# Block-sparse attention and a gated FFN on one core: 256-query attention units woven into the FFN one unit behind, probabilities as the stationary operand, tanh for sigmoid

## The chip, the cores and the metric

The kernel runs on one core of a Trainium2 chip. The time is device time in microseconds (us) of one launch, from the first to the last instruction and what the launch adds around it; the profiled execution is one such launch. A core has a TensorE (PE; its weight loads are listed apart as PEld), a VectorE (DVE), a ScalarE (ACT), a GpSimd (POOL, which here only issues loads) and a SyncE (SP, which issues stores). In some stretches TensorE was granted half of its clock, and this is said where it matters.

## The reference, cut to what matters

```python
B, H, S, D = 4, 8, 768, 64                        # attention
scores = q @ k.T / 8                              # per batch and head, 768 x 768
scores = where(mask, scores, -1e9)                # mask of 24 x 24 blocks of 32: band, edges, 3 random
attn   = exp(scores - max) / (sum + 1e-9)
x      = (attn @ v)  -> [3072 tokens, 512]        # heads side by side
gate   = 1 / (1 + exp(-(x @ w_gate)))             # 512 x 1536
out    = (gate * (x @ w_val)) @ w_out             # 1536 x 512, float32
```

Every token's FFN needs all 8 heads of that token, and nothing of other tokens. Neither kernel skips masked blocks: the mask is added in the score product by 24 extra contraction rows, so that a product has 64 + 24 = 88 rows.

## The kernel before

Attention runs head by head, then the FFN follows in six groups of 512 tokens. All operands on TensorE are fp16. In `matmul(out, stationary, moving)` the second operand is loaded as weights and the third streams past it.

```python
for b in range(B):
    for h in range(H):
        pt = ps.tile([128, S], f16, tag="pt", bufs=1)
        for o, src in ((0, q16[rb2]), (64, k16[rb2])):        # 12 transposes, 64 stationary columns
            for t in range(NJT):
                nc.tensor.transpose(pt[o : o + 64, t * 128 : (t + 1) * 128], src[:, h, t, :], ident)
        nc.vector.tensor_copy(qte[rq][0:64, :], pt[0:64, :])
        nc.vector.tensor_copy(kte[rq][0:64, :], pt[64:128, :])
        for t in range(NJT):                                  # 6 key tiles, 768 queries each
            st = ps.tile([128, 1024], f32, tag="st", bufs=2)
            nc.tensor.matmul(st[:, 0:512], ktile, qte[rq][0:88, 0:512], ...)
            nc.tensor.matmul(st[:, 512:768], ktile, qte[rq][0:88, 512:768], ...)
            nc.scalar.activation(ptile, st[:, 0:768], AF.Exp, bias=0.0, scale=SCALE)
        # one head later (phase B): v is stationary and carries a column of ones
        for i0, i1 in ((0, 512), (512, 768)):
            for t in range(NJT):
                nc.tensor.matmul(pv[:, 0:n], vex[rb2][:, h, t, :], pts[t][:, i0:i1], ...)
            nc.vector.tensor_copy(xT[kt][...], pv[0:64, 0:n])
            nc.scalar.activation(lnz[:, i0:i1], pv[64:65, 0:n], AF.Ln)      # the sums lie on one partition
        nc.scalar.activation(rz1, lnz, AF.Exp, bias=0.0, scale=-1.0)        # 1 / sum
        # one head later again (tail): spread 1/sum over 64 partitions, multiply
        nc.tensor.matmul(rbg[:, 0:n], ones464[0:1, :], rz1[:, i0:i1], ...)
        nc.vector.tensor_tensor(sl, sl, rbg[:, 0:n], op=ALU.mult)
# ... all attention done ...
for g in range(6):
    for f in range(12):
        # 4 matmuls into pg (x @ w_gate), 4 into pvv (x @ w_val), 512 columns each
        nc.scalar.activation(sg, pg, AF.Sigmoid)
        nc.vector.tensor_tensor(h_, sg, pvv, op=ALU.mult)
    # ... 4 x 12 matmuls with w_out, eviction, store
```

The softmax here doesn't subtract the row's maximum and nothing guards it: scores larger than these inputs give would overflow.

Of the kernel before, what the change touches and what calls it, by code (L numbers as in the profile page):

```python
# [13 lines left out]
ALU = mybir.AluOpType  # L15

B, H, S, D = 4, 8, 768, 64
BLK = 32
NB = S // BLK
NJT = S // 128  # L20
DM = H * D
DFF = 1536
NTOK = B * S
BIG = 1024.0
SCALE = 1.0 / 8.0
GT = 512
# [10 lines left out]
def kernel(  # L37
# [15 lines left out]
    _set_id = list(get_activation_tables(nc.m.arch)).index(  # L53
        "natural_log_exp_and_others"
    )
# [7 lines left out]
    e24_np = (np.arange(S)[None, :] // BLK == np.arange(NB)[:, None]).astype(np.float16)  # L63
# [7 lines left out]
    work = ctx.enter_context(tc.tile_pool(name="work", bufs=1))  # L71

    ident = sing.tile([128, 128], f16)
    nc.sync.dma_start(ident, ident_h.ap())
    e24 = sing.tile([NB, S], f16)
    nc.sync.dma_start(e24, e24_h.ap())
    ones464 = sing.tile([128, 64], f16)
    nc.vector.memset(ones464, 1.0)

    mb32 = sing.tile([NB, NB], f32)  # L80
    nc.sync.dma_start(mb32, mdet_h.ap())
    iota24 = sing.tile([NB, NB], f32)
    nc.sync.dma_start(iota24, iota_h.ap())
    sbi = sing.tile([NB, 3], mybir.dt.int64)
    nc.sync.dma_start(sbi, sampled_blocks)
    sbf = sing.tile([NB, 3], f32)
    nc.scalar.copy(sbf, sbi.bitcast(u16)[:, 0:12:4])
    for n in range(3):
        eqn = sing.tile([NB, NB], f32, tag=f"eq{n}", name=f"eq{n}")
        nc.vector.tensor_scalar(  # L90
            eqn, in0=iota24, scalar1=sbf[:, n : n + 1], scalar2=None, op0=ALU.is_equal
        )
        nc.vector.tensor_tensor(mb32, mb32, eqn, op=ALU.max)
    mb16 = sing.tile([NB, NB], f16)
    nc.vector.tensor_copy(mb16, mb32)  # L95

    mb24 = sing.tile([NB, S], f16)
    with tc.tile_pool(name="psmall", bufs=1, space=bass.MemoryType.PSUM) as psmall:
        p24 = psmall.tile([NB, 1024], f32)
        nc.tensor.matmul(p24[:, 0:512], mb16, e24[:, 0:512], start=True, stop=True)  # L100
        nc.tensor.matmul(p24[:, 512:768], mb16, e24[:, 512:768], start=True, stop=True)
        nc.vector.tensor_scalar(  # L102
            mb24,
            in0=p24[:, 0:768],
            scalar1=BIG,
            scalar2=BIG,
            op0=ALU.mult,
            op1=ALU.subtract,
        )

    wg = [sing.tile([128, DFF], f16, tag=f"wg{c}", name=f"wg{c}") for c in range(4)]
    wv = [sing.tile([128, DFF], f16, tag=f"wv{c}", name=f"wv{c}") for c in range(4)]
    wo = [sing.tile([128, DM], f16, tag=f"wo{f}", name=f"wo{f}") for f in range(12)]

    def _load_moe_weights():
        for c in range(4):
            nc.gpsimd.dma_start(wg[c], moe_w_gate[c * 128 : (c + 1) * 128, :])
            nc.gpsimd.dma_start(wv[c], moe_w_val[c * 128 : (c + 1) * 128, :])
        for f in range(12):
            nc.gpsimd.dma_start(wo[f], moe_w_out[f * 128 : (f + 1) * 128, :])  # L120

    xT = [sing.tile([128, NTOK], f16, tag=f"xT{c}", name=f"xT{c}") for c in range(4)]

    RQ = 4
    qte = [sing.tile([128, S], f16, tag=f"qte{r}", name=f"qte{r}") for r in range(RQ)]
    kte = [sing.tile([128, S], f16, tag=f"kte{r}", name=f"kte{r}") for r in range(RQ)]
    for r in range(RQ):
        nc.vector.tensor_copy(qte[r][64:88, :], mb24)
        nc.vector.tensor_copy(kte[r][64:88, :], e24)

    q16 = [
        sing.tile([128, H, NJT, 64], f16, tag=f"q16_{r}", name=f"q16_{r}")
        for r in range(2)
    ]
    k16 = [
        sing.tile([128, H, NJT, 64], f16, tag=f"k16_{r}", name=f"k16_{r}")
        for r in range(2)
    ]
    vex = [
        sing.tile([128, H, NJT, 65], f16, tag=f"vex{r}", name=f"vex{r}")  # L140
        for r in range(2)
    ]
    for r in range(2):
        nc.vector.memset(vex[r][:, :, :, 64:65], 1.0)

    out3 = out.rearrange("(g p) dm -> g p dm", p=128)
    CH = ((0, 512), (512, 768))

    def _moe_f(g, f, ps):
        t0 = g * GT  # L150
        pg = ps.tile([128, GT], f32, tag="pg", bufs=2)
        pvv = ps.tile([128, GT], f32, tag="pvv", bufs=2)
        for c in range(4):
            nc.tensor.matmul(  # L154
                pg,
                wg[c][:, f * 128 : (f + 1) * 128],
                xT[c][:, t0 : t0 + GT],
                start=(c == 0),
                stop=(c == 3),
            )  # L160
        for c in range(4):
            nc.tensor.matmul(  # L162
                pvv,
                wv[c][:, f * 128 : (f + 1) * 128],
                xT[c][:, t0 : t0 + GT],
                start=(c == 0),
                stop=(c == 3),
            )
        sg = work.tile([128, GT], f16, tag="sg", bufs=2)
        nc.scalar.activation(sg, pg, AF.Sigmoid)  # L170
        h_ = work.tile([128, GT], f16, tag=f"HT{f}", bufs=1, name=f"ht{f}")
        nc.vector.tensor_tensor(h_, sg, pvv, op=ALU.mult)
        return h_

    def _moe_out(g, tt, hts, ps):
        py = ps.tile([128, DM], f32, tag="py", bufs=2)
        for f in range(12):
            nc.tensor.matmul(  # L178
                py,
                hts[f][:, tt * 128 : (tt + 1) * 128],  # L180
                wo[f],
                start=(f == 0),
                stop=(f == 11),
            )
        ysb = work.tile([128, DM], f32, tag="ysb", bufs=2)
        nc.vector.tensor_copy(ysb, py)  # L186
        nc.sync.dma_start(out3[g * (GT // 128) + tt], ysb)

    pend = []
    stageB = []  # L190
    zbs = {}
    with tc.tile_pool(name="ps", bufs=1, space=bass.MemoryType.PSUM) as ps:
        for b in range(B):
            rb2 = b % 2
            for h0, h1 in (((0, 1), (1, H)) if b == 0 else ((0, H),)):
                nc.gpsimd.dma_start(
                    q16[rb2][:, h0:h1],
                    q[b, h0:h1].rearrange("h (t p) d -> p h t d", p=128),
                )
                nc.gpsimd.dma_start(  # L200
                    k16[rb2][:, h0:h1],
                    k[b, h0:h1].rearrange("h (t p) d -> p h t d", p=128),
                )
                nc.gpsimd.dma_start(
                    vex[rb2][:, h0:h1, :, 0:64],
                    v[b, h0:h1].rearrange("h (t p) d -> p h t d", p=128),
                )
            if b == 1:
                _load_moe_weights()
            for h in range(H):  # L210
                gh = b * H + h
                rq = gh % RQ
                pt = ps.tile([128, S], f16, tag="pt", bufs=1)
                for o, src in ((0, q16[rb2]), (64, k16[rb2])):
                    for t in range(NJT):
                        nc.tensor.transpose(  # L216
                            pt[o : o + 64, t * 128 : (t + 1) * 128],
                            src[:, h, t, :],
                            ident,
                        )  # L220
                nc.vector.tensor_copy(qte[rq][0:64, :], pt[0:64, :])
                nc.vector.tensor_copy(kte[rq][0:64, :], pt[64:128, :])  # L222
                pts = []
                for t in range(NJT):
                    st = ps.tile([128, 1024], f32, tag="st", bufs=2)
                    ktile = kte[rq][0:88, t * 128 : (t + 1) * 128]
                    nc.tensor.matmul(  # L227
                        st[:, 0:512], ktile, qte[rq][0:88, 0:512], start=True, stop=True
                    )
                    nc.tensor.matmul(  # L230
                        st[:, 512:768],
                        ktile,
                        qte[rq][0:88, 512:768],
                        start=True,
                        stop=True,
                    )
                    ptile = work.tile([128, S], f16, tag=f"PT{t}", bufs=3, name=f"pt{t}")
                    nc.scalar.activation(  # L238
                        ptile, st[:, 0:768], AF.Exp, bias=0.0, scale=SCALE
                    )  # L240
                    pts.append(ptile)
                def _phaseB(b=b, h=h, rb2=rb2, pts=pts, gh=gh):
                    kt, hh = h // 2, h % 2
                    lnz = work.tile([1, S], f32, tag="lnz", bufs=3)
                    for i0, i1 in CH:
# [82 lines left out]
```

## Time and profile before

| | before |
|---|---|
| time, median (lowest to highest) | 416.27 us (416.21 to 417.53, 4 runs) |
| first exponential | 15.1 us |
| one head of attention, steady | 6.27 us |
| one matmul of 512 columns in the FFN | 215 ns from start to start |

The head's 6.27 us is the distance between the first exponentials of neighbouring heads in the trace. First, the head of the profile page and its chain of waits: the work that ended last, followed back from the last instruction, as shares of the span.

```profile
span 417.8 us, 5146 instructions
PE 391.4 (94%) x2082; PEld 184.9 (44%) x2082; DVE 178.9 (43%) x307; ACT 239.7 (57%) x363; POOL 39.5 (9%) x39
PE 61%; ACT 33%; DVE 3%; issue 1%; DMA 0%; SPq 0%
```

Then the busy-time table: one stretch of attention, two between the stages and one of the FFN. The columns are the stretch, its length, and busy us (number of instructions) by engine, then TensorE's granted clock (PEclk, 1.00 is full), and what the DMAs did.

```profile
core 0: us, PE busy (x) PEld busy (x) DVE busy (x) ACT busy (x) POOL busy (x), PEclk, DMA share, GB/s
80.00:100.00 20.00, 19.40 (x123) 9.62 (x120) 10.67 (x20) 19.32 (x30) 0.00 (x0) 1.00 0.00 1
210.00:220.00 10.00, 8.49 (x31) 4.08 (x30) 2.54 (x5) 6.73 (x10) 0.00 (x0) 0.68 0.00 0
220.00:230.00 10.00, 7.32 (x23) 2.42 (x21) 3.64 (x7) 3.86 (x6) 0.00 (x0) 0.66 0.00 0
300.00:350.00 50.00, 50.00 (x233) 22.69 (x232) 17.89 (x26) 10.75 (x18) 0.00 (x0) 1.00 0.08 32
```

The two middle rows are the seam between the stages: the last exponential ends at 216.2 us, the first FFN product starts at 224.5, and the clock was half for 13.7 us between 209.6 and 230.1.

### The profile page before, as it was taken

How to read it: one execution, taken by the hardware profiler on the slowest of the kernel's cores; microseconds unless marked ns; L12 is line 12 of the kernel's file. 1: busy time of each engine (PE TensorE's matmuls, PEld its weight loads, DVE VectorE, ACT ScalarE, POOL GpSimd, SP SyncE). 2: the span in 40 equal slices, each digit the busy share in tenths (PEclk: the TensorE clock that was granted, in tenths of full speed). 3: DMA queues.
4: the chain of work that ended last, by engine and by line, in shares of the span. 5: the costliest groups of instructions: out<-in, count | busy, mean ns of one | idle time of the engine just before them, and what ended most of it. 6: DMA issues, size and time to landing. Idle time of an engine off the chain costs nothing.

```text
span 417.8 us, 5146 instructions
## 1 busy us (share of the span) xinstructions
PE 391.4 (94%) x2082; PEld 184.9 (44%) x2082; DVE 178.9 (43%) x307; ACT 239.7 (57%) x363; POOL 39.5 (9%) x39
## 2 busy tenths in 40 slices
PE   0799999999999999999987999999999999999996
PEld 0454444444444444444432444444444444444442
DVE  6445555555555555555523333333332332332431
ACT  1399999999999999999973320320321321321320
POOL 8253362002120000000000000000000000000000
PEclk9999999999999999999966999999999999999999
DMA  9999999900997000000000002002002002002002
GB/s 86 145 147 160 213 169 154 69 2 0 147 55 26 1 2 0 2 0 2 0 0 0 2 1 102 0 0 102 0 2 100 1 2 100 0 2 100 0 2 100
DMA packets 80614, 20.84 MB, mean 50 GB/s; under 512 B 74936, under 2 KB 76496, under 8 KB 80592
## 3 DMA queue, kind: packets, MB, share of 16 engines
q0 software_dynamic: 76848, 14.16, 58.9%
q1 hardware_dynamic: 3744, 6.37, 4.0%
q8 instruction: 16, 0.26, 0.3%
q14 instruction: 6, 0.05, 0.0%
HBM read 28.39 MB, written 6.29 MB: 83 GB/s over the span
## 4 chain that ended last, share of the span: by engine, by line
PE 61%; ACT 33%; DVE 3%; issue 1%; DMA 0%; SPq 0%
PE pg L154 15%; PE pvv L162 15%; PE py L178 15%; ACT lnz L260 6%; PE st L227 6%; PE pv L249 3%; PE rbg L268 2%; PE pt L216 2%; PE st L230 2%; DVE xT_119 L278 1%; DMA e_64<-bb_e 0%; DVE eq_76 L90 0%; DVE mb_85 L95 0%; DVE mb_87 L102 0%; ACT pt_2203 L238 0%
## 5 line engine op out<-in xcount | busy, mean ns | idle before, releaser
L170 ACT ACTIVATE sg<-pg 128x512 f16<-128x512 f32 x72 | 43.0, 597 | 134.5 <-PE pg L154 134.5
L186 DVE COPY ysb<-py 128x512 f32<-128x512 f32 x24 | 16.6, 691 | 45.2 <-PE py L178 45.2
L249 PEld LDWEIGHTS <-vex_141 128*65 128x65 f16 x192 | 22.0, 115 | 18.1 <-issue 8.4
L260 ACT ACTIVATE lnz<-pv 1x512 f32<-1x512 f32 x64 | 27.5, 474 | 3.1 <-DVE xT_119 L256 2.4
L154 PE MATMUL pg<-xT_116,wg_96 128*128 128x512 f16 x72 | 27.8, 385 | 0.5 <-DVE xT_119 L278 0.5
L249 PEld LDWEIGHTS <-vex_140 128*65 128x65 f16 x192 | 21.4, 113 | 15.3 <-issue 5.0
L162 PE MATMUL pvv<-xT_116,wv_100 128*128 128x512 f16 x72 | 27.8, 386 | 0.0
L154 PE MATMUL pg<-xT_117,wg_97 128*128 128x512 f16 x72 | 27.8, 386 | 0.0
L154 PE MATMUL pg<-xT_118,wg_98 128*128 128x512 f16 x72 | 27.8, 386 | 0.0
L154 PE MATMUL pg<-xT_119,wg_99 128*128 128x512 f16 x72 | 27.8, 386 | 0.0
L162 PE MATMUL pvv<-xT_117,wv_101 128*128 128x512 f16 x72 | 27.6, 383 | 0.0
L162 PE MATMUL pvv<-xT_118,wv_102 128*128 128x512 f16 x72 | 27.5, 383 | 0.0
L162 PE MATMUL pvv<-xT_119,wv_103 128*128 128x512 f16 x72 | 27.5, 382 | 0.0
L227 PE MATMUL st<-qte_120,kte_124 88*128 88x512 f16 x48 | 19.8, 413 | 1.7 <-DVE kte_124 L222 1.3
L227 PE MATMUL st<-qte_123,kte_127 88*128 88x512 f16 x48 | 18.6, 388 | 0.8 <-ACT pt_2352 L238 0.2
L227 PE MATMUL st<-qte_122,kte_126 88*128 88x512 f16 x48 | 18.4, 383 | 0.5
L227 PE MATMUL st<-qte_121,kte_125 88*128 88x512 f16 x48 | 18.4, 383 | 0.4
L256 DVE CAST xT_119<-pv 64x512 f16<-64x512 f32 (+1 forms) x16 | 8.6, 550 | 17.7 <-PE pv L249 17.6
L268 PEld LDWEIGHTS <-ones_66 1*64 1x64 f16 x64 | 6.3, 101 | 21.1 <-issue 19.0
L256 DVE CAST xT_116<-pv 64x512 f16<-64x512 f32 (+1 forms) x16 | 8.5, 549 | 13.6 <-PE pv L249 13.6
L256 DVE CAST xT_117<-pv 64x512 f16<-64x512 f32 (+1 forms) x16 | 8.6, 550 | 12.7 <-PE pv L249 12.7
L256 DVE CAST xT_118<-pv 64x512 f16<-64x512 f32 (+1 forms) x16 | 8.6, 550 | 12.7 <-PE pv L249 12.7
(760 smaller groups left out, 861.8 us busy)
## 6 DMA issues: line engine op xcount, KB each, us to landing
out_dram<-ysb SPq DMA_DIRECT2D x24, 256.0 KB, 2.0
q_1_137<-in_q_dram POOLq DMA_DIRECT2D x2, 768.0 KB, 10.0
k_1_139<-in_k_dram POOLq DMA_DIRECT2D x2, 768.0 KB, 12.0
vex_141<-in_v_dram POOLq DMA_DIRECT2D x2, 768.0 KB, 11.3
q_0_136<-in_q_dram POOLq DMA_DIRECT2D x1, 768.0 KB, 9.5
k_0_138<-in_k_dram POOLq DMA_DIRECT2D x1, 768.0 KB, 12.7
vex_140<-in_v_dram POOLq DMA_DIRECT2D x1, 768.0 KB, 12.2
q_0_136<-in_q_dram POOLq DMA_DIRECT2D x1, 672.0 KB, 8.7
```

The source lines that it names most:

```text
L154: nc.tensor.matmul(pg, wg[c][:, f * 128 : (f + 1) * 128], xT[c][:, t0 : t0 + GT], start=(c == 0), stop=(c == 3),)
L162: nc.tensor.matmul(pvv, wv[c][:, f * 128 : (f + 1) * 128], xT[c][:, t0 : t0 + GT], start=(c == 0), stop=(c == 3),)
L170: nc.scalar.activation(sg, pg, AF.Sigmoid)
L178: nc.tensor.matmul(py, hts[f][:, tt * 128 : (tt + 1) * 128], wo[f], start=(f == 0), stop=(f == 11),)
L186: nc.vector.tensor_copy(ysb, py)
L216: nc.tensor.transpose(pt[o : o + 64, t * 128 : (t + 1) * 128], src[:, h, t, :], ident,)
L227: nc.tensor.matmul(st[:, 0:512], ktile, qte[rq][0:88, 0:512], start=True, stop=True)
L230: nc.tensor.matmul(st[:, 512:768], ktile, qte[rq][0:88, 512:768], start=True, stop=True,)
L249: nc.tensor.matmul(pv[:, 0:n], vex[rb2][:, h, t, :], pts[t][:, i0:i1], start=(t == 0), stop=(t == NJT - 1),)
L256: nc.vector.tensor_copy(xT[kt][hh * 64 : hh * 64 + 64, b * S + i0 : b * S + i1], pv[0:64, 0:n],)
L260: nc.scalar.activation(lnz[:, i0:i1], pv[64:65, 0:n], AF.Ln)
L268: nc.tensor.matmul(rbg[:, 0:n], ones464[0:1, :], rz1[:, i0:i1], start=True, stop=True,)
```

## The change

Four things at once, by its intent:

1. Attention works in units of 256 queries of one batch (12 units), four head pairs each, six key tiles (slots) per pair. The FFN of a unit becomes possible when its four pairs are done; its matmuls are dealt out between the slots of the units that follow, by a running credit of 0.65 us of FFN per slot.
2. In the value product the probabilities are stationary (128 keys by 128 queries) and v streams past (65 columns). The sums then lie one to a query partition, so that a reciprocal and a multiplication on VectorE normalise. The logarithms, the one-partition exponential and the broadcast product fall away; x has to be transposed instead.
3. sigmoid(z) = 0.5 (1 + tanh(z/2)), so that one activation table serves for all.
4. Token p·6+t stands in partition p, tile t, so that loads read 1536 contiguous bytes in place of 256.

The order of instructions is fixed by hand. Core of the diff (declarations, loads and mask cut):

```diff
-    _set_id = list(get_activation_tables(nc.m.arch)).index("natural_log_exp_and_others")
+    _set_id = list(get_activation_tables(nc.m.arch)).index("exp_and_others")
...
+    def prep(src, dst, b, p, t0=0, t1=NT, evac=None):
+        pr = work.tile([128, NT, 2, D], f16, tag="pr", bufs=3, name="pr")
+        nc.vector.tensor_copy(pr[:, t0:t1, :, :], src[...].rearrange("a h t d -> a t h d"))
+        tp = ps.tile([128, 1024], f16, tag="m", bufs=2, name="tpq")
+        for t in range(t0, t1):
+            nc.tensor.transpose(tp[...], pr[:, t, :, :], ident)          # both heads of the pair at once
+        for a in range(2):
+            nc.vector.tensor_copy(dst[b % 2][0:D, 2 * p + a, ...], tp[a * D : (a + 1) * D, 0:n])
...
+    def qk(b, u, p, t):
+        st = ps.tile([128, 2, UQ], f32, tag="s", bufs=3, name="st")
+        # 2 matmuls of 256 columns, then exp of 128 x 512
+        nc.scalar.activation(pt, st, AF.Exp, bias=0.0, scale=SCALE)
...
+        def pv(self, i):                                                  # i = 0..3: query half, head
+            for t in range(NT):
+                nc.tensor.matmul(
+                    self.acc[:, s, a, :],
+                    self.pts[t][:, a, s * 128 : (s + 1) * 128],
+                    vex[self.b % 2][:, 2 * self.p + a, t, :], ...)
+        def norm(self):
+            nc.vector.reciprocal(rz, self.acc[:, :, :, D : D + 1])
+            nc.vector.tensor_tensor(self.x16, self.acc[:, :, :, 0:D], rz.broadcast_to(...), op=ALU.mult)
...
+        # FFN: th = tanh(pg[:, 0] / 2);  ht = (th + 1) * pg[:, 1];  y * 0.5 at the eviction
+                self.py = ps.tile([128, DM], f32, tag="y", bufs=1, name="py")
...
+    for p in range(NP):                                                   # all four pairs before the first score
+        mask_rows(0, 2 * p, 2 * p + 2)
+        prep(k16, kT, 0, p)
+        prep(q16, qT, 0, p, 0, 2)
+        vcopy(0, 2 * p, 2 * p + 2)
...
+            for t in range(NT):
+                pts.append(qk(b, u, p, t))
+                # t = 1..4: value product of the pair before;  t = 0: transpose of the pair before that
+                if t in (2, 5) and todo:
+                    todo.popleft()()                                      # prepare the next batch
+                give(0.65)                                                # FFN of the unit behind
```

## The prediction

> **What bounds the kernel now.** Two stages in series. In the busy-time table, every 20 us from 40 to 200 us has ScalarE busy 19.1 to 19.3 us: attention is ScalarE-bound. There the chain of waits alternates exponentials (0.81 us, 128x768), two logarithms (0.59, 0.36 us) and a one-partition exponential (0.82 us); the last three cost 57 us for 32 heads. From 230 to 415 us TensorE never idles: 300 to 350 us holds 233 matmuls, 215 ns per 512 columns, so 864 FFN matmuls need 186 us, while ScalarE is idle 134 us (sigmoid waiting for the gate product).
>
> **What the change does.** It fills TensorE's slack in attention with the FFN; TensorE becomes the one limit.
>
> - ScalarE, per unit of 256 queries: 24 exponentials of 128x512 (0.60 us by the sigmoid of that size) and 12 tanh of 128x256 (about 0.38 us): 19 us; 227 us in all.
> - TensorE: scores keep their 147,456 columns, 576x109 ns = 63 us. FFN 1152x109 ns + 288x216 ns = 188 us. Transposes 288x56 ns = 16 us. The broadcast product (10 us) goes. The value product becomes 1152 matmuls of 65 columns, each with its own 128-column weight load. The Trainium skill, "TensorE: Matmul & The Clock Gate", section on weight-path perf modes, says 128 columns of a non-FP32 type load fast; the trace agrees so far that 128-column loads take 99 ns and 65-column ones 115 ns. The pair's spacing isn't in the trace; I estimate 45 ns (35 to 65): 52 us against 62 before. Sum about 319 us.
> - VectorE: normalisation and two copies move here. About 0.42 us per slot (one key tile of one head pair), 0.9 where the next batch is prepared, against a slot of 1.07 us: not the limit, but TensorE waits for it.
>
> **The sum.**
> - Start: all four pairs' copies, transposes, evictions (0.55 us per 64x768) and mask rows precede the first score. About 4 us of VectorE per pair from about 10 us on: first exponential near 26 us (15 us before).
> - 30 slots without FFN (unit 0 and a quarter of unit 1), ScalarE/VectorE-bound: 22 us.
> - 258 slots of 0.22 scores + 0.18 value product + 0.02 + 0.65 FFN = 1.07 us: 276 us.
> - Preparing batches 1 to 3: 8 us of transposes and about 0.5 us of waiting for VectorE in each of 24: 20 us.
> - One y buffer: 12 waits of 0.5 us: 6 us.
> - Tail: the last value product, 21 us of FFN, last store: 25 us.
>
> Total about 372 us, 11% less.
>
> **What will show it.** ScalarE about 60% busy throughout; the chain of waits almost all TensorE; the last FFN unit alone at the end. Value-product spacing near 45 ns decides the largest term: 10 ns is 11 us. First exponential near 26 us. In each batch's middle unit TensorE waits for the pair copy.
>
> **What would make it wrong.** Weight loads that don't hide behind 65-column matmuls (80 ns or more: plus 40 us, still faster). A start slowed by VectorE operations stretched while the DMA descriptors are written (before, 24x24 operations took 1.8 us at 6 us). FFN weights arriving late for the first unit (14 MB by 55 us; before never exceeds 213 GB/s): plus 5 to 10 us. Weight loads wholly hidden (30 ns), few waits: 345 us.
>
> Range 348 to 396 us. Faster by over 2%: 0.96; within 2%: 0.03; slower: 0.01.

## More of the kernel before

The piece of the chain that covers one head shows that neither engine was alone on the path (columns: start, us, what):

```profile
59.53 0.81 ACT pt_642 L238
60.34 0.72 ACT rz_616 L262
61.06 0.70 ACT pt_647 L238
61.80 0.38 PE st L227
62.28 0.33 PE rbg L268
62.61 0.23 PE pt L216 x2
62.84 0.32 PE st L227
63.16 0.12 PE st L230
63.31 0.81 ACT pt_662 L238
64.12 0.77 ACT pt_667 L238
64.92 0.85 ACT lnz L260 x2
65.80 0.81 ACT pt_737 L238
```

From 61.8 to 63.3 us the path runs through TensorE: a score product, the broadcast product, transposes, scores again.

## The result

| | before | changed |
|---|---|---|
| median | 416.27 us | 371.18 us (369.34 to 371.94, 4 runs) |
| ratio | | 0.8891, 95% interval 0.8854 to 0.8928 |

Ratios here are the mean time of one kernel's fast runs over that of the other's fast runs of the same rounds, so they are not quite the ratio of the medians quoted. The changed kernel is 11% faster, at 371.18 us against 372 predicted.

The same lines of the page after the change:

```profile
span 370.2 us, 8135 instructions
PE 322.2 (87%) x3458; PEld 254.4 (69%) x3458; DVE 178.7 (48%) x458; ACT 214.6 (58%) x433; POOL 26.9 (7%) x37
PE 76%; DMA 11%; DVE 7%; POOL 2%; ACT 2%; issue 1%; ACTq 0%; POOLq 0%
```

The busy-time table, one stretch in which nothing is prepared and one in which batch 3 is:

```profile
180.00:200.00 20.00, 19.64 (x214) 15.41 (x213) 6.99 (x19) 13.75 (x28) 0.00 (x0) 1.00 0.08 28
220.00:240.00 20.00, 17.69 (x214) 15.44 (x213) 12.55 (x32) 12.78 (x28) 0.00 (x0) 1.00 0.04 15
```

ScalarE is no longer near its limit, and nothing of the two-stage picture is left. The timeline of TensorE within two slots shows the terms of the steady part (start, us, then the instructions, merged):

```profile
200.45 0.38 PE L202 MATMUL st<-qT,kT 88*128 88x256 f16 x2
200.67 0.36 PE L224 MATMUL pv<-vex,pt 128*128 128x65 f16 x6
200.87 0.60 PE L262 MATMUL pg<-xT,wv 128*128 128x256 f16 x4
201.30 0.38 PE L202 MATMUL st<-qT,kT 88*128 88x256 f16 x2
```

Two score products take 0.22 us, six pairs of weight load and value product 0.20 us (33 ns each), four FFN products 0.43 us. What interrupts this is in the table of waits for TensorE (engine, tile, line, who it waited for: us in total, times, longest):

```profile
PE tpq L184 <- DVE pr L178: 29.7, 22, 3.2
PE p L154 <- DVE mb L151: 6.5, 1, 6.5
PE py L285 <- DVE ysb L294: 6.0, 12, 0.9
```

The first line is the pair copy: 20.9 us of it fall before 51 us (start, unit 0 and the first pair of unit 1), 8.8 us in the merged part. And the start, on the timeline: the first score product waits in TensorE's queue behind the transposes of all four pairs, which wait for VectorE.

```profile
9.39 0.36 DVE L178 COPY pr<-k 128x768 f16<-128x768 f16 x1
...
14.94 0.53 DVE L178 COPY pr<-k 128x768 f16<-128x768 f16 x1
...
20.18 0.36 DVE L178 COPY pr<-k 128x768 f16<-128x768 f16 x1
...
25.12 0.43 DVE L178 COPY pr<-k 128x768 f16<-128x768 f16 x1
...
28.64 3.04 ACT L210 ACTIVATE pt<-st 128x512 f16<-128x512 f32 x6 [26.62 <-PE st L202]
```

The four pairs begin about 5.2 us apart. In this first part TensorE was slow: until 42.4 us its matmuls start 0.83 to 0.84 ns a column apart, later 0.43 to 0.49, and 0.83 again from 52.7 to 56.1 us, where half the clock is on record. The clock records begin only at 42.4 us (21.9 us in the kernel before, with the same spacing until then), so the 1.00 that the clock column prints for this part is no reading. The predicted sum against the trace, by the stretches of the prediction:

| term | predicted, us | in the trace, us | how read |
|---|---|---|---|
| start, to the first exponential | 26 | 28.6 | timeline |
| 30 slots without FFN | 22 | 22.5 | to the first score of unit 1's second pair, 51.1 us |
| 258 slots with FFN (276), preparation (20), waits for y (6) | 302 | 289.8 | to the end of the last slot's FFN, 340.9 us |
| tail | 25 | 29.3 | to the end, 370.2 us |
| sum | 375 | 370.2 | |

The terms of the prediction in fact add up to 375; its text says "about 372".

### The profile page after: what moved, and what is told of

Its sections match the earlier page's. It is cut to its first block, busy times and chain, and to the rows that moved or that the text cites. A ratio compares the mean times of both kernels' runs of the same rounds, so it can differ in the third digit from the quotient of the medians.

```text
span 370.2 us, 8135 instructions
## 1 busy us (share of the span) xinstructions
PE 322.2 (87%) x3458; PEld 254.4 (69%) x3458; DVE 178.7 (48%) x458; ACT 214.6 (58%) x433; POOL 26.9 (7%) x37
## 4 chain that ended last, share of the span: by engine, by line
PE 76%; DMA 11%; DVE 7%; POOL 2%; ACT 2%; issue 1%; ACTq 0%; POOLq 0%
PE pg L262 33%; PE py L285 17%; PE st L202 14%; PE pv L224 9%; DMA q<-in_q_dram 6%; DMA wg<-in_moe_w_gate_dram 4%; PE tpq L184 3%; DVE ysb L294 3%; DVE ht L272 2%; DMA k<-in_k_dram 2%; ACT th L271 2%; PE tpx L246 1%; DVE pr L178 1%; POOL q L101 0%; POOL wg L111 0%
## 5 line engine op out<-in xcount | busy, mean ns | idle before, releaser
L210 ACT ACTIVATE pt<-st 128x512 f16<-128x512 f32 x288 | 169.4, 598 | 103.4 <-PE st L202 102.5
L202 PE MATMUL st<-qT,kT 88*128 88x256 f16 x576 | 113.5, 281 | 0.1
L272 DVE SCALAR_TENSOR_TENSOR ht<-th,pg 128x256 f16<-128x256 f32 x144 | 60.6, 421 | 91.3 <-ACT th L271 91.1
L262 PE MATMUL pg<-xT,wg 128*128 128x256 f16 x576 | 86.9, 273 | 1.1 <-DVE xT L249 0.9
L262 PE MATMUL pg<-xT,wv 128*128 128x256 f16 x576 | 86.8, 273 | 0.0
L285 PE MATMUL py<-wo,ht 128*128 128x512 f16 x288 | 75.7, 378 | 6.0 <-DVE ysb L294 6.0
L271 ACT ACTIVATE th<-pg 128x256 f32<-128x256 f32 x144 | 55.2, 383 | 41.9 <-PE pg L262 40.0
L202 PEld LDWEIGHTS <-kT 88*128 88x128 f16 x576 | 56.9, 101 | 24.8 <-issue 1.7
L224 PE MATMUL pv<-vex,pt 128*128 128x65 f16 x1152 | 69.4, 196 | 0.0
L224 PEld LDWEIGHTS <-pt 128*128 128x128 f16 x1152 | 63.1, 99 | 6.2 <-DVE qT L188 0.4
L285 PEld LDWEIGHTS <-ht 128*128 128x128 f16 x288 | 24.3, 97 | 22.1 <-issue 7.5
L188 DVE COPY kT<-tpq 64x768 f16<-64x768 f16 x32 | 17.7, 554 | 13.4 <-PE tpq L184 13.2
```

The lines of the kernel that those rows point to most:

```text
L188: nc.vector.tensor_copy(dst[b % 2][0:D, 2 * p + a, t0 * 128 : t1 * 128], tp[a * D : (a + 1) * D, 0:n],)
L202: nc.tensor.matmul(st[:, a, :], kT[b % 2][0:KR, h, t * 128 : (t + 1) * 128], qT[b % 2][0:KR, h, u * UQ : (u + 1) * UQ], start=True, stop=True,
L210: nc.scalar.activation(pt, st, AF.Exp, bias=0.0, scale=SCALE)
L224: nc.tensor.matmul(self.acc[:, s, a, :], self.pts[t][:, a, s * 128 : (s + 1) * 128], vex[self.b % 2][:, 2 * self.p + a, t, :], start=(t == 0),
L262: nc.tensor.matmul(self.pg[:, i, :], w[:, c, f * 128 : (f + 1) * 128], self.xT[:, c, :], start=(c == 0), stop=(c == 3),)
L271: nc.scalar.activation(th, self.pg[:, 0, :], AF.Tanh, bias=0.0, scale=0.5)
```

## The experiments

Twelve kernels ran, in three sets. The changed kernel (371.18 us) is the base of most; each set ran the kernel before beside it, whose medians were 416.85, 416.83 and 416.62 us. The changed kernel was not run again, so differences to it compare with its first four runs.

### Does TensorE set the pace? Two doublings

`pv_twice` computes each value product twice:

```diff
-            for t in range(NT):
+            for t in 2 * list(range(NT)):
                 nc.tensor.matmul(self.acc[:, s, a, :], self.pts[t][...], vex[...], start=(t == 0), stop=(t == NT - 1))
```

> The changed kernel with every value product computed twice (1152 more weight loads and 65-column matmuls; the result is the same, no other engine gets work). Theory, TensorE sets the pace and a pair of weight load and matmul costs 33 ns (what the trace of the changed kernel suggests): 1152 x 33 = +38 us, 409 us. If the predicted 45 ns were right: +52 us, 423 us. Rival, ScalarE or the latency between engines sets the pace: well under 20 us more.

Measured: 403.19 us (402.14 to 403.62), ratio to before 0.9663 (0.9611 to 0.9715): 32.0 us more than the changed kernel. Divided by 1152, a pair costs 28 ns in time, a little under the 33 ns between its starts, as a part of it fills waits. A unit without preparation went from 25.0 to 27.9 us (distance of first exponentials), which is 2.9 us / 96 = 30 ns. The predicted 45 ns is refuted, and TensorE's work shows nearly whole in the time.

`tanh_twice` gives ScalarE 55 us more and TensorE nothing:

```diff
-                nc.scalar.activation(th, self.pg[:, 0, :], AF.Tanh, bias=0.0, scale=0.5)
+                for _ in range(2):
+                    nc.scalar.activation(th, self.pg[:, 0, :], AF.Tanh, bias=0.0, scale=0.5)
```

> The changed kernel with every tanh computed twice: 144 x 0.38 = 55 us more of ScalarE, no work for other engines. Theory, TensorE sets the pace in the 258 slots with FFN (ScalarE 0.79 us of a 1.12 us slot before, 0.98 with the second tanh): under 12 us more, most of it in the last unit, where the tanh lies on the path. Rival, ScalarE sets the pace of the merged part: +40 to +55 us.

Measured: 380.49 us (379.37 to 382.06), 9.3 us more for 55 us of work. In the profiled executions (7.4 us apart) the last exponential starts 5.0 us later and the stretch after it is 2.4 us longer. ScalarE doesn't set the pace; the longer path from gate product to `ht` costs a little. The two runs together decide for TensorE.

### What is the merging worth?

`serial` keeps every new piece but lets the FFN units run after all attention:

```diff
-                        f_ = Ffn(done.b, done.u, done.xT)
-                        ffn_parts.extend(f_.parts())
+                        later.append((done.b, done.u, done.xT))
...
+    for args in later:
+        ffn_parts.extend(Ffn(*args).parts())
+        give(1e6)
```

> The changed kernel with its merging undone: the FFN units run after all attention (12 buffers for x transposed in place of 3), everything else as it is. Theory, the merging is what makes the new pieces pay: 28 us start, 288 slots at about 0.62 us of ScalarE = 179, then 12 FFN units at 17.5 us (as the last unit of the changed kernel took alone) = 210: 415 to 425 us, no faster than the kernel before. Rival, the gain comes from the lighter ScalarE and TensorE work and not from the merging: 380 us or less.

Measured: 425.29 us (421.93 to 428.41; the longest run is of the slow state, the three fast ones have a median of 422.93), ratio to before 1.0169 (1.0079 to 1.026, fast runs alone): slightly slower than before, whether by 2% is unclear, and 52 us slower than the changed kernel by the fast runs. Attention lasts from 29 to 207 us, and the twelve FFN units then take 17.7 us each, with one accumulator for y (9.4 us of waits in all) and two for the gate waiting for evictions that merging hides. In the profiled run the clock was half in five stretches between 53 and 152 us, some 31 us in all; what that adds is not separated. So the new attention and the new FFN, in series, gain nothing; they gain when each fills the waits of the other. A clean attention unit in this run takes 11.6 us, 0.48 us a slot, although one exponential lasts 0.60 us: back to back they overlap. The Trainium skill, "ScalarE: Activation LUTs", section "What ACT_TABLE_LOAD costs", says that back-to-back activations overlap by about 93 ns; here it is 0.12 us (0.478 from start to start, 0.597 long). The theory counted 0.62 us a slot, and was right on the total because the units that prepare a batch took up to 19.0 us.

### Was ScalarE the limit of attention before?

`before_nolog` takes the logarithms and the one-partition exponential from the kernel before (wrong result):

```diff
-                        nc.scalar.activation(lnz[:, i0:i1], pv[64:65, 0:n], AF.Ln)
...
-                    nc.scalar.activation(rz1, lnz, AF.Exp, bias=0.0, scale=-1.0)
+                    rz1 = rconst          # memset once to 1/256
```

> The kernel before with only its two logarithms and the one-partition exponential per head taken away (wrong result on purpose: every head is scaled by a constant; the broadcast product and its multiplication stay). Theory, ScalarE bounds attention alone: a head falls from 6.27 us to about 5.0 us (6 exponentials of 0.81 = 4.9; TensorE needs about 4.8): 32 x 1.27 = 40 us less, 376 us, as much as the whole change gives. Rival, TensorE's order and waits bind as soon as ScalarE gets lighter: under 25 us less.

Measured: 404.54 us (404.38 to 404.68), ratio 0.9699 (0.9649 to 0.9749): 12 us less, not 40. The rival holds. A head falls only from 6.27 to 6.02 us (mean of two: they alternate 5.6 and 6.4), which is 8 us for 32 heads; the rest of the gain lies outside the steady heads, in the profiled executions (15.6 us apart) 2.0 us before the first exponential and 6.6 us after the last head began. The busy-time table of the same stretch:

```profile
80.00:100.00 20.00, 20.00 (x128) 10.47 (x126) 11.02 (x20) 15.12 (x21) 0.00 (x0) 1.00 0.01 1
```

And the chain of waits of the whole run:

```profile
PE 94%; DMA 3%; POOL 1%; DVE 1%; issue 0%; ACT 0%; ACTq 0%; POOLq 0%
```

ScalarE is at 15.1 of 20 and off the chain, and TensorE has taken over. But its columns explain only part of 6.02 us: scores 4608, value product 4608, transposes 1536, broadcast 768 columns are 11,520, or 4.8 us at the FFN's 215 ns for 512. Where is the rest? The timeline of TensorE in the kernel before shows it:

```profile
200.96 0.27 PE L230 MATMUL st<-qte_121,kte_125 88*128 88x256 f16 x1
201.16 0.24 PE L216 MATMUL pt<-ident,q_1_137 128*64 128x128 f16 x1
...
201.35 0.22 PE L216 MATMUL pt<-ident,q_1_137 128*64 128x128 f16 x1
201.50 0.39 PE L227 MATMUL st<-qte_121,kte_125 88*128 88x512 f16 x1
```

The score product of 256 columns is followed after 0.20 us, not 0.11, where the next matmul has 64 stationary columns, and a transpose by a score product after 0.15, not 0.06. Over 40 to 160 us of `before_nolog` the start times of consecutive matmuls give medians of 202 ns for 256-column score to transpose, against 108 to a value product, and of 152 ns for transpose to score. All changes of shape together (64-column transposes; broadcast product with one contraction row and 64 columns) are about nine a head, 93 to 116 ns each. The Trainium skill, "TensorEngine Tiling (Array Packing)", section "Tiling Modes", key properties, says that changing the tiling mode drains the TensorE; it gives no time for it. `wide_nolog` tests this: q and k side by side, one 128-column transpose for both, 128 columns of ones.

```diff
-        for o, src in ((0, q16[rb2]), (64, k16[rb2])):
-            for t in range(NJT):
-                nc.tensor.transpose(pt[o : o + 64, t * 128 : (t + 1) * 128], src[:, h, t, :], ident)
+        for t in range(NJT):
+            nc.tensor.transpose(pt[:, t * 128 : (t + 1) * 128], qk16[rb2][:, h, t, :, :], ident)
...
-    ones464 = sing.tile([128, 64], f16)
+    ones464 = sing.tile([128, 128], f16)
...
```

> The run before_nolog (kernel before without its logarithms, wrong result on purpose) with q and k side by side in one tile, so that one 128-column transpose serves both (6 a head in place of 12 of 64 columns), and the ones of the broadcast product widened from 64 to 128 columns. Theory: what kept TensorE at 6.02 us a head there is the change between matmuls with 64 and with 128 stationary columns: score to transpose starts 202 ns apart in place of 108, transpose to score 152 in place of 56, about nine such changes of 95 ns a head. Without them TensorE needs about 4.7 us and the exponentials 4.9: 5.0 us a head, 404.5 - 32 x 1.0 = 372 us. Rival, the 6.02 us come from waits between the engines (score buffers, evictions): 395 us or more.

Measured: 383.62 us (382.95 to 385.03): 20.9 us less than `before_nolog`, 5.29 us a head (mean of two: they alternate 4.6 and 6.0). TensorE now starts a transpose 0.11 us after the score product, where there were 0.20:

```profile
86.27 0.27 PE L225 MATMUL st<-qte,kte 88*128 88x256 f16 x1
86.38 0.33 PE L213 MATMUL pt<-ident,qk 128*128 128x128 f16 x3
...
87.02 0.33 PE L213 MATMUL pt<-ident,qk 128*128 128x128 f16 x3
87.28 0.28 PE L260 MATMUL rbg<-rconst,ones 1*128 1x256 f16 x1
87.49 0.41 PE L243 MATMUL pv<-pt,vex 128*65 128x512 f16 x1
```

The rival is refuted, and the theory's 372 us was too low by 12. The broadcast product still has one contraction row: the last transpose to it takes 149 ns from start to start, not 56, and it takes 208 ns to the next value product, not 109. Four such changes a head, by these figures, are about 0.4 us, which would cover the missing 0.3; that part was not tested. Part of the 0.72 us gained is the shorter row of transposes (6 in place of 12, in two column halves that partly overlap), so the run shows both together. An estimate from the traces parts them: 768 columns less are 0.32 us at the FFN's rate, and what the start-to-start times hold beyond their columns fell from 1.17 to 0.77 us a head, which is the other 0.40.

`before_wide` is the same edit with the logarithms kept and the result right.

> The kernel before, logarithms kept, with the same wide transposes and wide ones (right result). Theory: ScalarE still needs 6.2 us a head, so the lighter TensorE gains next to nothing alone: 411 to 417 us. Rival: TensorE was the tighter limit of the two, 395 us or less.

Measured: 418.22 us (416.46 to 419.84), ratio 1.0025 (0.9969 to 1.008): nothing gained, and 1 us above the expected range. Each limit hides the other: ScalarE's part alone gives 12 us, TensorE's part alone nothing, both 33 us.

### Is tanh needed, and what does the token order give?

`sigmoid` puts the sigmoid back into the changed kernel (and takes the 0.5 and the added 1 out).

> The changed kernel with the sigmoid in place of tanh (0.5 and the added 1 taken out too; right result). Theory: sigmoid and exponential don't share a table, so each change reloads one at 1.28 us, about 2 x 144 reloads when they alternate: ScalarE 215 + 370 = 585 us, and the time follows: 580 to 640 us. Rival: the reloads overlap or are grouped, under 450 us.

Measured: 668.73 us (2 runs, 667.57 and 669.90), above the expected range; the groups of instructions name the cost:

```profile
L271 ACT ACT_TABLE_LOAD x131 | 168.1, 1283 | 2.3
L210 ACT ACT_TABLE_LOAD x130 | 166.8, 1283 | 2.4
```

These are 261 reloads, 335 us of ScalarE. TensorE's granted clock averaged 0.746 over the span, which the expectation had not counted; that its waits for ScalarE brought the clock down is not shown. The Trainium skill, "ScalarE: Activation LUTs", puts a load at about 1283 ns (section "What ACT_TABLE_LOAD costs") and lists exp and tanh in one set (section "Table sets: the hidden batching unit"); the trace agrees to the nanosecond, and the changed kernel has one load in all. This merging without tanh would have lost.

`tok_natural` undoes the token order alone.

```diff
-TOK = (np.arange(S) % 128) * NT + np.arange(S) // 128
+TOK = np.arange(S)
...
-            src[b, h0:h1].rearrange("h (p t) d -> p h t d", t=NT)[:, :, t0:t1, :],
+            src[b, h0:h1].rearrange("h (t p) d -> p h t d", t=NT)...   # partial loads split by tile
...                                                                     # the store likewise
```

> The changed kernel with the token order put back: q, k and v are read in pieces of 256 bytes, not 1536 (partial q loads are split by key tile, because a load has at most three dimensions: 7 more issues). Theory: [...] batch 1, which lands at 50 us and holds TensorE there, lands 8 to 12 us later: 376 to 384 us. Rival, the loads are hidden and the start is VectorE's: under 3 us.

Measured: 378.72 us (378.03 to 379.61), 7.5 us more. In the profiled executions, which differ by 5.8 us, unit 0 begins 1.6 us later and takes 1.0 us longer, and unit 1 takes 32.2 us in place of 29.1; the rest is as long. In unit 1 the pair copy waits 1.10 us for the load of k of batch 1 and 2.21 us for that of q, where the changed kernel waits 0.20 us for q, and TensorE idles 3.41 us behind the second. The seven additional issues are part of the run, so a share of the later start may be theirs. The Trainium skill, "DMA: Bandwidth & Descriptors", specifications, names 512 bytes as the least transfer for line rate; here loads moved 203 to 206 GB/s from 20 to 60 us with 1536-byte pieces, and with 256-byte ones fell to about 155 GB/s from 47 us on, while batch 1 came in.

### Taking away the waits that are left

Three edits aim at the pair copies, the y accumulator and the start. `pr_early` issues the pair copy two slots before its transposes:

```diff
...
+                if t in (0, 3) and todo and len(todo[0]) > 1:
+                    pair_copy(*todo[0][1:])
                 if t in (2, 5) and todo:
-                    todo.popleft()()
+                    todo.popleft()[0]()
```

> The changed kernel with the pair copy on VectorE issued two slots before the transposes that read it. Theory: TensorE no longer waits 0.5 to 1.0 us for it in most of the 24 preparations of batches 1 to 3; 10 to 15 us less, 356 to 361 us. Rival: the wait is filled by what TensorE owes anyway, or comes back as a wait for the evictions of these transposes: under 4 us.

Measured: 357.98 us (356.89 to 360.05), ratio to before 0.8576: 13.2 us less than the changed kernel, as expected. TensorE's wait for pair copies in the merged part falls from 8.8 to 2.3 us; in the profiled executions (11.9 us apart) units 1 to 8 take 9.5 us less and unit 0, where the half clock ended at 37.1 us in place of 42.4, takes 2.4 us less.

`two_y` gives y a second accumulator, taken from the scores:

```diff
-        st = ps.tile([128, 2, UQ], f32, tag="s", bufs=3, name="st")
+        st = ps.tile([128, 2, UQ], f32, tag="s", bufs=2, name="st")
...
-                self.py = ps.tile([128, DM], f32, tag="y", bufs=1, name="py")
+                self.py = ps.tile([128, DM], f32, tag="y", bufs=2, name="py")
```

> The changed kernel with two output accumulators in PSUM in place of one, and two score buffers in place of three. Theory: the 12 waits for the eviction of y (0.37 to 0.78 us) go, 4 to 6 us less, 366 us, and two score buffers are enough because the exponential has a 1.1 us slot to free one. Rival: the third score buffer is needed, slower by 5 us or more.

Measured: 364.77 us (362.72 to 365.53), 6.4 us less. The wait for y is gone, and the two score buffers cost 0.5 us of waits in the whole run.

`start_order` prepares only pair 0 before the first score:

```diff
-    for p in range(NP):
-        mask_rows(0, 2 * p, 2 * p + 2)
-        prep(k16, kT, 0, p); prep(q16, qT, 0, p, 0, 2); vcopy(0, 2 * p, 2 * p + 2)
+    first_k(0); first_q(0)                  # the same for pair 0 alone
...
+            for p in range(1, NP):
+                todo.append(lambda p=p: first_k(p)); todo.append(lambda p=p: first_q(p))
...
-            todo.append(lambda: mask_rows(1, 0, H))
...  (not code: second buffer's mask rows go with batch 1, whose preparation starts in unit 1's last pair, 8 items for 12)
```

> The changed kernel with only pair 0 prepared before the first score; pairs 1 to 3 of batch 0, and the second buffer's mask rows, are prepared between the slots of units 0 to 2. Theory, the start is VectorE's queue (about 4 us for each pair): first exponential near 14 us in place of 28.6, unit 0 then bound by VectorE at about 4.2 us a pair, and FFN begins 10 to 16 us earlier; part is lost again because weights and batch 1 arrive at the same rate as before (about 204 GB/s until 63 us): 356 to 364 us. Rival, the loads set the start: under 4 us gained.

Measured: 371.79 us (369.97 to 372.37): nothing, as the rival has it, but not for its reason. The first exponential came at 13.9 us, 14.8 us sooner, and unit 2 still began 9.7 us sooner. Then it went, unit by unit (distances of first exponentials, us):

| | first exp | unit 0 | unit 1 | unit 2 | unit 3 | unit 4 | unit 5 |
|---|---|---|---|---|---|---|---|
| changed | 28.6 | 18.4 | 29.1 | 27.0 | 25.0 | 31.2 | 25.5 |
| start_order | 13.9 | 23.9 | 28.7 | 33.5 | 25.0 | 27.0 | 30.3 |
| all_three | 14.0 | 19.1 | 23.2 | 27.4 | 24.5 | 25.2 | 26.0 |

Unit 0, in which pairs 1 to 3 are now prepared, takes 5.5 us longer, and unit 2 6.6 us. From 13 to 80 us no engine that computes waited for a load, so the rival's reason is not it. In unit 2, where batch 1 is now prepared, TensorE waits 4.6 us for pair copies, in four waits; the longest, 1.94 us, stands behind mask rows in VectorE's queue:

```profile
77.75 0.55 DVE L168 COPY qT<-mb 24x1536 f16<-24x1536 f16 x1
78.23 0.54 DVE L168 COPY kT<-e 24x1536 f16<-24x1536 f16 x1
78.78 0.36 DVE L178 COPY pr<-k 128x768 f16<-128x768 f16 x1
...
79.20 0.51 PE L184 MATMUL tpq<-ident,pr 128*128 128x128 f16 x6 [1.94 <-DVE pr L178]
```

The granted clock was half from 26.1 to 39.8 us, but that does not set this run apart: by the spacing of its matmuls the changed kernel, too, ran at half rate until 42.4 us.

`all_three` puts the three edits together.

> The three edits together (start order, two y accumulators, early pair copy). Theory, they act in different stretches and add up: 371 - 11 - 5 - 10 = 345 us, 340 to 352. Rival, they overlap: 352 to 360 us.

Measured: 337.24 us (336.29 to 337.51), ratio to before 0.8072 (0.8038 to 0.8105), result right: 33.9 us less than the changed kernel, below the expected range. Alone they gave 13.2, 6.4 and -0.6, together 19.0; the remaining 14.9 is put down to the earlier start (14.7 us between the first exponentials), which is kept once the copy is early. That is by subtraction, as no run has the other two edits without it; the traces agree: unit 2 begins 16.9 us sooner than in `pr_early`, and the earlier start holds to the end. The wait of TensorE for pair copies is what fell, from 24.3 us in `start_order`:

```profile
PE tpq L191 <- DVE pr L178: 4.0, 3, 2.4
```

The clock is on record as full from 27.9 us to the end; before that the matmuls start 0.83 to 0.84 ns a column apart here too. This version beats both kernels.

## Why the prediction was right, point by point

- **The total, 372 against 371.18, and the direction.** Right. The structure was right as well: TensorE sets the pace (`pv_twice`, `tanh_twice`), and merging is what pays (`serial`). That the total fits to 1 us is luck: against terms that add up to 375, the slots came 12 us shorter and the start and the tail 7 us longer.
- **"I estimate 45 ns (35 to 65): 52 us".** Mis-sized, and outside its own range: 33 ns from start to start, 38 us for 1152. The prediction doesn't say how it came to 45. The 128-column load, 98 ns long by itself, is nearly hidden: the columns of a 65-column matmul alone take 27 ns at the FFN's rate of 0.42 ns a column (65 x 0.42). This made the slots 12 us cheaper than predicted: 96 x 12 ns = 1.15 us for each of about 10.75 units.
- **"First exponential near 26 us".** 28.6; the pairs took 5.2 us each, not 4, since transposes and evictions take turns and don't overlap: VectorE idles 0.9 and 0.5 us in each pair for transposes, which ran at half rate.
- **"30 slots without FFN (unit 0 and a quarter of unit 1), ScalarE/VectorE-bound: 22 us".** 22.5 us, but the reason isn't borne out. From 28.0 to 47.1 us ScalarE was busy 12.7 us and VectorE 11.8 of 19.1; two copies of mask rows (29.3 to 33.1 us) held TensorE for 2.9 us, and its matmuls ran at half rate until 42.4 us. That the size fits is partly luck.
- **"about 0.5 us of waiting for VectorE in each of 24".** Right in mean: batches 2 and 3 cost 6.6 and 6.4 us over clean units of 25.0 us, 2.7 us of which is their 48 transposes, so about 0.5 us for each of eight.
- **"One y buffer: 12 waits of 0.5 us: 6 us".** Right: 12 waits, 6.0 us; removing them gave 6.4.
- **"Tail: ... 25 us".** 29.3. The lone last unit waits for the gate's two accumulators (two gate and value tiles take 1.96 us where 1.75 are TensorE's) and twice for y, and the store comes after.
- **"FFN weights arriving late".** Did not happen. The nearest thing is batch 1's q, which stands behind the weights in the load queue: its pair copy waited 0.20 us for it at 50.3 us. The 11% of DMA in the chain of waits are not lost time either: where the last wait was for a load, the chain is followed back along the whole load (22.0 us here), however short the wait. With the old token order this did become a wait.
- **"attention is ScalarE-bound" and "It fills TensorE's slack in attention".** Wrong as a reading, though the total didn't suffer from it. It took 97% busy on ScalarE for the one limit, and the logarithms and their exponential for 57 us of time (the sum of their durations; ScalarE's busy time fell by 47 us without them). Their removal is worth 12 us in all, 8 of them in the steady heads, because TensorE needs 6.02 of the 6.27 us of a head. The change pays since its TensorE work is smaller as well: attention falls from 6.02 x 32 = 193 us to about 117 us. (Estimate from measured spacings: 12 units of 48 x 109 + 96 x 33 + 8 x 56 ns, and 192 transposes of 56 ns.) It has no matmuls with 64 stationary columns and no one-row broadcast, and the value product has 65 columns where there were 128 for the same work. The prediction had put TensorE's saving at 20 us (10 for the value product, 10 for the broadcast), and reached the right time because it added up the new kernel and didn't subtract from the old.

The changed kernel gives a part back: 14 us at the start and some 19 us in waits, which the last run recovered.

## What to carry to other kernels

Predict a restructured kernel by adding up the new one on its slowest engine, stretch by stretch, and add the waits; subtracting the "freed" 57 us of ScalarE from the old one would have been wrong by 45 us here. When two engines both look full, test them by taking work from each alone and from both, since each hides the other. Order work for an in-order engine so that its inputs were started some slots before, and judge an earlier start only after the waits behind it are gone: the same edit gave nothing alone and, by subtraction, 15 us with the copies early.

## What the Trainium skill lacked or had wrong

- "TensorEngine Tiling (Array Packing)", "Tiling Modes": says that changing the tiling mode drains the TensorE, without a size. Here a matmul with 64 stationary columns next to one with 128 cost about 95 ns at each change (202 against 108 ns, 152 against 56 ns; 65 columns next to 128 cost nothing, 108 ns after a 256-column score), and a product with one contraction row about 100 ns each way; nine changes a head.
- "TensorE: Matmul & The Clock Gate", "Back-to-back issue gap": gives about 81 ns per matmul at N=128 for a stream of loads and matmuls. Here pairs of a 128-column fp16 load and a 128-column transpose started 56 ns apart, and pairs with 65 columns 33 ns apart; the formula of the isolated gap, N/2.4 + 2.5 ns, fits better (55.8 and 29.6 ns).
- "Perfetto Trace Analysis", "Identifying the Most-Contended Engine": takes occupancy as a fair measure for ScalarE. Here 97% occupancy in attention stood beside a gain of 3% of the time for removing 57 us of its durations, as activations overlap by 0.12 us and TensorE was as close to its limit (6.02 of a head's 6.27 us).
- "ScalarE: Activation LUTs": the 1283 ns of a table load and the shared set of exp and tanh were confirmed.
